# A fused attention, two-layer network and gated unit on one core: four PSUM buffers for the first batch's V tiles, and the output weights split inside the gated unit

## The chip, the cores and the metric

The kernel runs on one NeuronCore of a Trainium2 chip. The metric is the device time of one execution in microseconds. The engines are named as in the profile: PE (TensorE matmuls), PEld (its weight loads), DVE (VectorE), ACT (ScalarE), POOL (GpSimd) and SP (SyncE, which here only issues DMAs).

## What is computed

Three stages follow each other: windowed attention over 4 batches, 8 heads, 576 positions and head size 64; a layer norm with a two-layer network (512 to 2048 to 512, ReLU, residual); and a gated unit. The part of the reference that this change touches is the gated unit:

```
h = x @ w_in
h = 0.5 * h * (1.0 + np.tanh(c * (h + 0.044715 * h ** 3)))
u, v = h[..., :512], h[..., 512:]
v_n = (v - mu) / np.sqrt(var + 1e-06) * g_ln
v_s = np.einsum('ts,bsd->btd', w_sg, v_n) + b_sg[None, :, None]
return x + (u * v_s) @ w_out
```

mu and var are taken over the 512 features of v. x has 4 batches of 576 rows and 512 columns; w_in is 512 x 1024, w_sg 576 x 576, w_out 512 x 512.

## The kernel before, in words

Every product of float32 matrices is made of three products of shorter numbers: each operand is split into a high part (ACT copies it to a rounded type) and a low part (POOL, or DVE, subtracts the high part from the source). The names of these pairs end in h and l. Weights arrive as 64-bit floats and pass a longer split first (class `Split64`): ACT line 76, DVE lines 81, 83, 85 and 88, ACT line 92 for the high part, POOL line 93 for the low part.

**Phase 1** (`phase1`) does attention and the two-layer network. A planner (`Sched`) plays the engines forward with assumed costs and priorities and so writes the order of instructions on each engine. The last work of phase 1 on PE are the products of line 796 into the tiles `acc` (two halves of 12 matmuls each for the last piece), which DVE scales (line 735, `et`) and adds to x (line 739); two DMAs (line 742) bring that x to DRAM. It is the ninth group of rows, and it holds the last 64 rows ("tail") of all four batches.

**Phase 2** (`Phase2`) is the gated unit. Its weights are loaded and split by jobs (`Job`), in the order wv, wu, the first rows of x, ws, wo. When attention is over, `end_attention` hands all jobs to the planner (`flow`), so that their steps fill gaps of phase 1. It also hands it two early V tiles (`early_v`): V tile i is the product of 128 rows of x with wv, 12 matmuls of 512 columns on line 1037 (`v_products`), into one of the two buffers of the PSUM pool `ps_v`. The constants `EPRI` place these two among the last steps of phase 1.

Behind phase 1 the order is that of the code (`Phase2.run`). `play` takes a list of chunks. For each it issues the chunk's matmuls, then one further step of every chunk that is still pending, then so many ticks of the job queue (`tick`: at most one step of each active job, and one new load). The chunks are

- `v_tile`, three steps: *first* (ACT square line 1069, DVE line 1070, ACT tanh line 1071), *stats* (DVE lines 1074, 1088, 1089, 1090, then POOL's power on line 1091) and *norm* (DVE line 1094, then the split into vn: ACT line 1028, POOL line 1029). Line 1074 is the last reader of the PSUM buffer. V tile 4 is the tail of two batches; its parts are called vt.
- `u_chunk`, 24 matmuls on line 1113 over all 576 rows of x, in a buffer of the pool `ps_u` (three buffers); then the same *first*, and DVE line 1074 into u.
- `vs_chunk` (SG), 28 matmuls on line 1130 into a `ps_u` buffer, each chunk reading all of vn and vt; then DVE lines 1134 and 1137 (the gate) and a split into gh and gl.
- `out_chunk` (O), 24 matmuls on line 1158 from gh, gl and wo, then DVE line 1164 and the DMA of the output.

`first_tail` splits the tail of batch 0 straight from SBUF: into x2h and x2l (64 rows, read by every U chunk) and into xth and xtl (128 rows, read by V tile 4). For batch 1 and later the rows of x come back from DRAM by jobs (`x2_jobs`, `tail_jobs`), which queue behind wo's. Of batch 0 the order of chunks is V0 V1, then `first_tail`, then V2 V3 U0 V4 U1 U2 U3 with two ticks behind each, then SG 0 to 3 with two ticks each.

Of the kernel before, what the change touches and what calls it, by code (L numbers as in the profile page):

```python
# [7 lines left out]
F32 = mybir.dt.float32  # L8
# [6 lines left out]
PSUM = bass.MemoryType.PSUM  # L15
# [3 lines left out]
DM, DF, DG = 512, 2048, 512  # L19
# [24 lines left out]
LBACK = 14, 26  # L44
OB, OC = 3, 0
LQ = 1, 0, 3, 2, 4, 8
EPRI = (-1, 9)

NF = 3
SNAKE = ((0, 0), (1, 0), (1, 1), (0, 1), (2, 0), (2, 1), (2, 2), (0, 2), (1, 2), (1, 3), (0, 3), (2, 3))  # L50
# [14 lines left out]
class Split64:  # L65
# [25 lines left out]
    def last(self, h, l):  # L91
        self.nc.scalar.activation(out=h, in_=self.x, func=ACTF.Copy)
        self.nc.gpsimd.tensor_tensor(out=l, in0=self.x, in1=h.bitcast(F32), op=ALU.subtract)
# [105 lines left out]
class Unit:  # L199


    def __init__(self, run, i):
        self.run, self.i = run, i
        self.last = i == run.i1 - 1
# [17 lines left out]
def phase1(tc, nc, a, x2d, cst, p2):  # L222
# [99 lines left out]
    need = {}  # L322
# [520 lines left out]
    def end_attention():  # L843
        yield Op(None, 0, 0, need=[("ev", s.n) for s in runs] + [("w", n) for n in range(40)], token="attention")
        for p in (P["st"], raw, ap2, ps_s, ps_o, ps_t):
            p.release()
        p2.ps_v = tc.alloc_tile_pool(name="ps_v", bufs=2, space=PSUM, side="right", reuse_waits="tile")
        p2.open_0()
        sched.done["p2", "wv"] = sched.now
        for n, j in enumerate(list(p2.queue)):  # L850
            sched.spawn(p2.flow(sched, j, n), sched.now)
        for i in range(2):
            sched.spawn(p2.early_v(i, when[2, stream[-1]] + EPRI[i]), sched.now)

    for e in units:
# [3 lines left out]
    for gen in ([warm(), constants()] + [load_wide(slice(x, y), t) for x, y, t in LW]  # L859
                + [moe(), open_split(), last_quarter(), end_attention()]  # L860
                + [weights(n) for n in range(40)] + [norm(g) for g in range(G)]
                + [load(s) for s in runs if not s.wide] + [scores(s) for s in runs] + [burst(s) for s in runs if s.n >= KB] + [unit(e) for e in units]):
        sched.spawn(gen)
# [41 lines left out]
class Phase2:  # L905
# [122 lines left out]
        nc.scalar.activation(out=h, in_=src, func=ACTF.Copy)  # L1028
        nc.gpsimd.tensor_tensor(out=l, in0=src, in1=h.bitcast(F32), op=ALU.subtract)  # L1029

    def v_products(self, i):
        xs = self.xtail if i == 4 else self.x
        c0 = 0 if i == 4 else i * 128
        ps = self.ps_v.tile([128, DG], F32, tag="v", name="ps_v")
        for kc in range(4):
            for x, (s, m) in enumerate(((0, 0), (0, 1), (1, 0))):
                self.nc.tensor.matmul(ps, xs[s][:, kc, c0:c0 + 128], self.wv[m][:, kc], start=kc == 0 and x == 0,  # L1037
                                      stop=kc == 3 and x == 2)
        return ps

    def early_v(self, i, pri):

        yield Op("PE", 2560, pri, need=[("sc2", n) for n in range(4)] + [("st2", 8)])
        self.early[0, i] = self.v_products(i)

    def run(self, x8, left):
        tc, nc, a, x2d = self.tc, self.nc, self.a, self.x2d
        wu, wo, ws, xtail, bb, g2 = self.wu, self.wo, self.ws, self.xtail, self.bb, self.g2
# [3 lines left out]
        vn = self.pair(wp, [128, 4, DG], "vn")  # L1052
        tp = self.open("p2a", 3)
        bp = self.open("p2b")
        ps_u = tc.alloc_tile_pool(name="ps_u", bufs=3, space=PSUM, reuse_waits="tile")
        self.vt = {}
        K1 = 0.044715
        KC = float(np.sqrt(2.0 / np.pi))
# [1 line left out]
        def gelu2(ps, shape):  # L1060

            t = tp.tile([128, S], F32, tag="ge", name="ge")
            n = int(np.prod(shape))
            t = t[:, :n]
            if len(shape) == 2:
                t = t.rearrange("p (a b) -> p a b", a=shape[0])

            def first():
                act.activation(out=t, in_=ps, func=ACTF.Square)
                dve.scalar_tensor_tensor(out=t, in0=t, scalar=1.0 / K1, in1=ps, op0=ALU.add, op1=ALU.mult)  # L1070
                act.activation(out=t, in_=t, func=ACTF.Tanh, scale=K1 * KC)  # L1071

            def last(out):
                dve.scalar_tensor_tensor(out=out, in0=t, scalar=1.0, in1=ps, op0=ALU.add, op1=ALU.mult)

            return first, last

        def v_tile(b, i):

            ps = self.early.pop((b, i)) if (b, i) in self.early else self.v_products(i)  # L1080
            first, last = gelu2(ps, [DG])
            t = tp.tile([128, DG], F32, tag="vg", name="vg")
            ag = tp.tile([128, 2], F32, tag="ba", name="ba")

            def stats():
                st = tp.tile([128, 6], F32, tag="bs", name="bs")
                last(t)
                dve.bn_stats(out=st, in_=t)
                dve.bn_aggr(out=ag, in_=st)
                dve.tensor_scalar(ag[:, 1:2], ag[:, 1:2], 4e-6, None, ALU.add)  # L1090
                pool.tensor_tensor(out=ag[:, 1:2], in0=ag[:, 1:2], in1=mh, op=ALU.pow)

            def norm():
                dve.tensor_scalar(t, t, ag[:, 0:1], ag[:, 1:2], ALU.subtract, ALU.mult)
                if i < 4:
                    self.split(vn[0][:, i], vn[1][:, i], t)
                else:
                    for z in range(2):
                        o = self.vt[b + z] = self.vtp[z]
                        hi, lo = slice(64 * z, 64 * z + 64), slice(64 - 64 * z, 128 - 64 * z)  # L1100
                        self.split(o[hi], o[lo], t[hi])

            return [first, stats, norm]
# [68 lines left out]
        def play(chunks, ticks=1):  # L1172


            for f, b, i in chunks:
                pend.append(f(b, i))
                for st in pend:
                    st.pop(0)()
                pend[:] = [st for st in pend if st]
                for z in range(ticks):  # L1180
                    self.tick()

        V = lambda b: [(v_tile, b, i) for i in range(5 if b % 2 == 0 else 4)]
        U = lambda b: [(u_chunk, b, d) for d in range(4)]
        SG = lambda b: [(vs_chunk, b, d) for d in range(4)]
        O = lambda b: [(out_chunk, b, d) for d in range(4)]
        play(V(0)[:2])
        self.first_tail(x8)
        for p in left:
            p.release()  # L1190
        gp = self.open("p2g", 2)
        load_res(0)
        self.need("wu")
        play([V(0)[2], V(0)[3], U(0)[0], V(0)[4]] + U(0)[1:], 2)
        self.need("ws")
        for b in range(B):
            nb = b + 1
# [10 lines left out]
            v, o = V(nb), O(b) if nb < B - 1 else []  # L1208
# [78 lines left out]
```

## Time and profile before

| what | value |
|---|---|
| median of three runs | 754.61 us (753.49 to 755.19) |
| the profiled execution's own time | 752.81 us |
| its span in the profile | 750.8 us |
| PE busy | 736.4 us, 98% of the span |
| DVE, ACT, POOL busy | 448.3, 308.5, 245.8 us |
| PE's share of the chain that ended last | 93% |

Busy time is the time in which an engine had an instruction in work, and PE's matmuls overlap, so that a matmul of 0.39 us can follow the one before after 0.23 us. The clock (PEclk) is the share of full speed that TensorE was granted. Times in the rows are microseconds from the start of the span.

### The profile page before, as it was taken

Reading aid. Unit: us, or ns where it says so; the run is one execution under the profiler, and the core shown is the slowest. Engines: PE = TensorE matmul, PEld = TensorE weight load, DVE = VectorE, ACT = ScalarE, POOL = GpSimd, SP = SyncE. Lnnn points to the kernel's source line nnn. Section 1 sums busy time; section 2 is a strip of 40 time slices with the busy share of each in tenths; the row PEclk is TensorE's granted clock in tenths of the full one; section 3 lists DMA queues with packets and bytes.
Section 4 is the critical chain, followed back from the end, with each engine's and each line's share of the span. In section 5 each row is a group of like instructions: output and inputs, shape, how many; then the busy total and the mean of one; then the engine's idle time right before and its main releaser. Section 6 shows DMA issues by size and latency. Waiting matters only on the chain.

```text
span 750.8 us, 15850 instructions
## 1 busy us (share of the span) xinstructions
PE 736.4 (98%) x6270; PEld 685.9 (91%) x6270; DVE 448.3 (60%) x1149; ACT 308.5 (41%) x795; POOL 245.8 (33%) x307
## 2 busy tenths in 40 slices
PE   7999999999999999999999999999899999999998
PEld 3669899999999999999999999999799999999997
DVE  6899889896643453453343438434966746647632
ACT  5896755544323323433323424233453334243410
POOL 2533432333313212222212423026356307327220
PEclk9999999999999999999999999999999999999999
DMA  8654631331121020021122234304500050160002
GB/s 296 220 176 117 190 106 34 92 106 51 56 89 52 25 69 26 27 85 29 28 66 58 71 90 131 124 30 139 183 24 2 31 173 0 48 206 0 1 33 94
DMA packets 51625, 63.41 MB, mean 84 GB/s; under 512 B 10336, under 2 KB 38880, under 8 KB 51552
## 3 DMA queue, kind: packets, MB, share of 16 engines
q1 hardware_dynamic: 51552, 62.41, 26.5%
q8 instruction: 49, 0.80, 0.4%
q14 instruction: 24, 0.20, 0.1%
HBM read 52.96 MB, written 9.44 MB: 83 GB/s over the span
## 4 chain that ended last, share of the span: by engine, by line
PE 93%; DVE 2%; DMA 1%; ACT 1%; POOL 1%; issue 1%; SPq 0%; DVEq 0%; POOLq 0%; ACTq 0%
PE ps_h L785 26%; PE acc L796 25%; PE ps_s L1130 8%; PE ps_u L1113 7%; PE ps_o L1158 7%; PE ps_v L1037 6%; PE o L622 5%; PE tps L582 3%; PE s L454 3%; PE ps_ln L701 1%; DMA st<-in_w 1%; PE ps_ln L644 1%; DMA st<-in_wo 1%; PE ps_w L356 1%; PE s L440 1%
## 5 line engine op out<-in xcount | busy, mean ns | idle before, releaser
L796 PE MATMUL acc<-hh,w2h 128*128 128x256 f32 x576 | 163.6, 284 | 0.0
L785 PE MATMUL ps_h<-xh,w1h 128*128 128x256 f32 x576 | 163.0, 283 | 0.0
L785 PE MATMUL ps_h<-xl,w1h 128*128 128x256 f32 x576 | 160.2, 278 | 0.0
L785 PE MATMUL ps_h<-xh,w1l 128*128 128x256 f32 x576 | 160.1, 278 | 0.0
L796 PE MATMUL acc<-hl,w2h 128*128 128x256 f32 x576 | 160.1, 278 | 0.0
L796 PE MATMUL acc<-hh,w2l 128*128 128x256 f32 x576 | 160.0, 278 | 0.0
L726 DVE SCALAR_TENSOR_TENSOR hl<-ps_h,hh 128x512 fp32r<-128x512 f32 x72 | 49.7, 690 | 127.3 <-ACT hh L724 127.0
L785 PEld LDWEIGHTS ps_h<-xh,w1h 128*128 128x128 f32 x576 | 108.6, 188 | 1.0 <-issue 0.9
L796 PEld LDWEIGHTS acc<-hh,w2h 128*128 128x128 f32 x576 | 108.7, 189 | 0.7 <-DVE sc L85 0.3
L796 PEld LDWEIGHTS acc<-hl,w2h 128*128 128x128 f32 x576 | 108.4, 188 | 0.2
L785 PEld LDWEIGHTS ps_h<-xl,w1h 128*128 128x128 f32 x576 | 108.4, 188 | 0.1
L785 PEld LDWEIGHTS ps_h<-xh,w1l 128*128 128x128 f32 x576 | 108.3, 188 | 0.0
L796 PEld LDWEIGHTS acc<-hh,w2l 128*128 128x128 f32 x576 | 108.3, 188 | 0.0
L724 ACT ACTIVATE hh<-ps_h 128x512 fp32r<-128x512 f32 x72 | 42.8, 595 | 138.8 <-PE ps_h L785 138.8
L463 POOL TENSOR_SCALAR_AFFINE_SELECT m<-m 128x256 f32<-128x256 f32 x100 | 44.7, 452 | 143.7 <-ACT m L543 141.6
L505 ACT ACTIVATE t<-t,sm 128x128 f32<-128x128 f32 x144 | 56.1, 394 | 14.6 <-DVE sm L499 14.6
L513 POOL TENSOR_TENSOR t<-t,sm 128x256 f32<-128x256 f32 x52 | 32.9, 633 | 42.4 <-DVE sm L509 34.9
L76 ACT ACTIVATE sc<-st 128x512 f32<-128x512 f32 (+1 forms) x52 | 30.9, 599 | 24.6 <-DMA st<-in_w 6.7
L1029 POOL TENSOR_TENSOR gl<-gt,gh 128x576 fp32r<-128x576 f32 x16 | 22.9, 1429 | 53.0 <-ACT gh L1028 53.0
L1071 ACT ACTIVATE ge<-ge 128x512 f32<-128x512 f32 (+1 forms) x34 | 22.4, 657 | 34.9 <-DVE ge L1070 34.9
L85 DVE SCALAR_TENSOR_TENSOR sc<-st,sc 128x512 int32<-128x512 int32 (+1 forms) x52 | 35.9, 692 | 0.3
L622 PE MATMUL o<-m,rv 128*64 128x128 f32 (+3 forms) x416 | 34.7, 296 | 0.3 <-POOL m L463 0.3
(163 smaller groups left out, 1530.5 us busy)
## 6 DMA issues: line engine op xcount, KB each, us to landing
st<-in_w SPq DMA_DIRECT2D x24, 512.0 KB, 4.2
x2d<-x SPq DMA_DIRECT2D x18, 256.0 KB, 2.0
out<-xr SPq DMA_DIRECT2D x15, 288.0 KB, 2.1
st<-in_w SPq DMA_DIRECT2D x16, 256.0 KB, 2.6
st<-in_wi SPq DMA_DIRECT2D x8, 512.0 KB, 3.9
st<-x2d SPq DMA_DIRECT2D x8, 512.0 KB, 5.1
xr<-x2d SPq DMA_DIRECT2D x8, 512.0 KB, 6.3
rq<-in_q SPq DMA_DIRECT2D x28, 128.0 KB, 3.2
```

The source lines that it names most:

```text
L85: dve.scalar_tensor_tensor(out=xi, in0=self.wh, scalar=-0x40000000, in1=xi, op0=ALU.bitwise_and, op1=ALU.bitwise_or)
L463: pool.affine_select(out=out, in_=in_, pattern=pat, compare_op=ALU.is_ge, fill=0.0, base=-1 if up else 0, channel_multiplier=1 if up else -1)
L505: act.activation(out=t[:, h], in_=t[:, h], func=ACTF.Exp, bias=st[:, h:h + 1], scale=-1.0, accum_out=sums[:, h, 0:1])
L622: pe.matmul(s.O[64 * h:64 * h + 64, oc:oc + w], v, s.M[m][0:k, h, mc:mc + w], start=x == 0, stop=x == len(mm) - 1, skip_group_check=True)
L724: act.activation(out=h, in_=ps, func=ACTF.Relu)
L726: dve.scalar_tensor_tensor(out=l, in0=ps, scalar=0.0, in1=h.bitcast(F32), op0=ALU.max, op1=ALU.subtract)
L785: pe.matmul(ps[:, half], w[:, kc, f], m[:, kc], start=kc == 0 and x == 0, stop=kc == 3 and x == 2)
L796: pe.matmul(accs[half][:, d], w[:, f, ds], m[:, k], start=fi and d == 0 and k == 0 and x == 0, stop=la and k == 1 and x == 2, skip_group_c ...
L1037: self.nc.tensor.matmul(ps, xs[s][:, kc, c0:c0 + 128], self.wv[m][:, kc], start=kc == 0 and x == 0, stop=kc == 3 and x == 2)
L1113: pe.matmul(ps[:, z, 0:288], wu[s][:, kc, ds], self.x[m][:, kc, 288 * z:288 * z + 288], start=kc == 0 and x == 0, stop=kc == 3 and x == 2)
L1130: pe.matmul(ps[:, z, 0:288], l, r[:, 288 * z:288 * z + 288], start=n == 0, stop=n == len(mm) - 1)
L1158: pe.matmul(ps[:, z, 0:288], wo[s][:, kc, ds], gated[b][m][:, kc, 288 * z:288 * z + 288], start=n == 0, stop=n == 11)
```

## The change

- `EPRI` has four entries, so four early V tiles are planned into the end of phase 1: V1, V2 and V3 directly one behind another. Tiles 0 and 1 of batch 0 go to a new PSUM pool `ps_e` of two buffers, tiles 2 and 3 to `ps_v`. V2 and V3 ask for the second part of x as well (`8 + i // 2`).
- `ps_u` is opened later, when `ps_e` has been released; it covers the same banks.
- The four wo jobs are left out of the planner's hands. They stay in the queue of `Phase2` and are done by its ticks, ahead of the jobs for batch 1's x.
- All four V tiles of batch 0 are played before `first_tail`, without ticks. The order behind it is U0 U1 V4 U2 U3.

```
-EPRI = (-1, 9)
+EPRI = (-1, 9, 10, 11)
...
-        for n, j in enumerate(list(p2.queue)):
+        p2.ps_e = tc.alloc_tile_pool(name="ps_e", bufs=2, space=PSUM, side="right", reuse_waits="tile")
+        for n, j in enumerate(z for z in list(p2.queue) if z.name != "wo"):
             sched.spawn(p2.flow(sched, j, n), sched.now)
-        for i in range(2):
+        for i in range(4):
             sched.spawn(p2.early_v(i, when[2, stream[-1]] + EPRI[i]), sched.now)
...
-    def v_products(self, i):
+    def v_products(self, b, i):
...
-        ps = self.ps_v.tile([128, DG], F32, tag="v", name="ps_v")
+        ps = (self.ps_e if b == 0 and i < 2 else self.ps_v).tile([128, DG], F32, tag="v", name="ps_v")
...
-        yield Op("PE", 2560, pri, need=[("sc2", n) for n in range(4)] + [("st2", 8)])
-        self.early[0, i] = self.v_products(i)
+        yield Op("PE", 2560, pri, need=[("sc2", n) for n in range(4)] + [("st2", 8 + i // 2)])
+        self.early[0, i] = self.v_products(0, i)
...
-        ps_u = tc.alloc_tile_pool(name="ps_u", bufs=3, space=PSUM, reuse_waits="tile")
...
-        play(V(0)[:2])
+        play(V(0)[:4], 0)
+        self.ps_e.release()
+        ps_u = tc.alloc_tile_pool(name="ps_u", bufs=3, space=PSUM, reuse_waits="tile")
         self.first_tail(x8)
...
-        play([V(0)[2], V(0)[3], U(0)[0], V(0)[4]] + U(0)[1:], 2)
+        play(U(0)[:2] + V(0)[4:] + U(0)[2:], 2)
```

The first place is ACT's row from the square of V1 to the square of V3 and the tail split. Of before (ps_v_7065 is V1, ps_v_7140 V2, ps_v_7168 V3; x2h<-x and xth<-x are the tail):

```order
L1069 ACTIVATE ge_7113<-ps_v_7065 128x512
L1071 ACTIVATE ge_7113<-ge_7113 128x512
L92 ACTIVATE woh_6935<-sc_7028 128x512
L1028 ACTIVATE x2h_6665<-x_5432 128x4x64
L1028 ACTIVATE xth_6937<-x_5432 128x512
L1028 ACTIVATE vnh_7095<-vg_7107 128x512
L1069 ACTIVATE ge_7153<-ps_v_7140 128x512
L1071 ACTIVATE ge_7153<-ge_7153 128x512
L1028 ACTIVATE vnh_7095<-vg_7114 128x512
L1069 ACTIVATE ge_7181<-ps_v_7168 128x512
```

The same place of ACT with the change (ps_v_7035 is V1, ps_v_7087 V2, ps_v_7115 V3, ps_u_7161 U0):

```order
L1069 ACTIVATE ge_7075<-ps_v_7035 128x512
L1071 ACTIVATE ge_7075<-ge_7075 128x512
L1029 ACTIVATE vnh_7061<-vg_7070 128x512
L1069 ACTIVATE ge_7100<-ps_v_7087 128x512
L1071 ACTIVATE ge_7100<-ge_7100 128x512
L1029 ACTIVATE vnh_7061<-vg_7076 128x512
L1069 ACTIVATE ge_7128<-ps_v_7115 128x512
L1071 ACTIVATE ge_7128<-ge_7128 128x512
L1029 ACTIVATE x2h_6668<-x_5432 128x4x64
L1029 ACTIVATE xth_6936<-x_5432 128x512
L1029 ACTIVATE vnh_7061<-vg_7101 128x512
L1069 ACTIVATE ge_7186<-ps_u_7161 128x576
```

The tail split has moved from behind V1's tanh to behind V3's tanh, and the last wo copy ahead of it is gone.

The second place is DVE between V4's line 1074 and its norm on line 1094. Of before (vg_7249 is V4):

```order
L1074 SCALAR_TENSOR_TENSOR vg_7249<-ge_7248,ps_v_7235 128x512
L1088 BN_STATS bs_7284<-vg_7249 128x6
L1089 BN_AGGR ba_7250<-bs_7284 128x2
L1090 TENSOR_SCALAR ba_7250<-ba_7250 128x1
L1070 SCALAR_TENSOR_TENSOR ge_7283<-ge_7283,ps_u_7258 128x576
L1094 TENSOR_SCALAR vg_7249<-vg_7249,ba_7250 128x512
```

And with the change (vg_7256 is V4; sc_7238 and sc_7265 belong to the first and second piece of wo):

```order
L83 TENSOR_SCALAR sc_7238<-sc_7238 128x512
L85 SCALAR_TENSOR_TENSOR sc_7238<-st_7199,sc_7238 128x512
L1074 SCALAR_TENSOR_TENSOR vg_7256<-ge_7255,ps_v_7242 128x512
L1088 BN_STATS bs_7293<-vg_7256 128x6
L1089 BN_AGGR ba_7257<-bs_7293 128x2
L1090 TENSOR_SCALAR ba_7257<-ba_7257 128x1
L1070 SCALAR_TENSOR_TENSOR ge_7292<-ge_7292,ps_u_7267 128x576
L88 SCALAR_TENSOR_TENSOR sc_7238<-st_7199,sc_7238 128x512
L81 TENSOR_SCALAR sc_7265<-sc_7265 128x512
L83 TENSOR_SCALAR sc_7265<-sc_7265 128x512
L85 SCALAR_TENSOR_TENSOR sc_7265<-st_7201,sc_7265 128x512
L1094 TENSOR_SCALAR vg_7256<-vg_7256,ba_7257 128x512
```

Seven instructions of the wo split (the two of the first piece above, its line 81 ahead of them, and four more) now stand between V4's line 1070 and its norm, where there was none.

The third place is ACT during SG, where batch 1's x is split. Of before (gh<-gt are the four gates, x2h<-st the parts of batch 1's x):

```order
L1028 ACTIVATE gh_7358<-gt_7389 128x576
L1028 ACTIVATE x2h_6665<-st_7393 128x4x256
L1028 ACTIVATE gh_7358<-gt_7426 128x576
L1028 ACTIVATE x2h_6665<-st_7395 128x4x256
L1028 ACTIVATE gh_7358<-gt_7464 128x576
```

With the change:

```order
L92 ACTIVATE woh_6934<-sc_7308 128x512
L1029 ACTIVATE gh_7353<-gt_7384 128x576
L92 ACTIVATE woh_6934<-sc_7351 128x512
L1029 ACTIVATE x2h_6668<-st_7391 128x4x256
L1029 ACTIVATE gh_7353<-gt_7427 128x576
L1029 ACTIVATE x2h_6668<-st_7396 128x4x256
L1029 ACTIVATE gh_7353<-gt_7468 128x576
```

The first part of batch 1's x now stands behind the last piece of wo, and that piece's DVE steps stand behind the first two gates.

## Rows read from the trace of the kernel before

**Rows 1.** The page's first part: busy us (share of the span) and instructions.

```profile
PE 736.4 (98%) x6270; PEld 685.9 (91%) x6270; DVE 448.3 (60%) x1149; ACT 308.5 (41%) x795; POOL 245.8 (33%) x307
```

**Rows 2.** PE's waits, whole span: us in total, times, longest.

```profile
PE ps_v L1037 <- DVE vg L1074: 3.2, 1, 3.2
```

**Rows 3.** Timeline of PE: start, us, instruction, idle before and its releaser.

```profile
533.38 0.28 PE L796 MATMUL acc<-hh,w2l 128*128 128x256 f32 x1
...
536.05 0.39 PE L1037 MATMUL ps_v<-wvh,x2l 128*128 128x512 f32 x1
539.68 0.50 PE L1037 MATMUL ps_v<-wvh,x2h 128*128 128x512 f32 x1 [3.25 <-DVE vg L1074]
...
546.89 0.42 PE L1113 MATMUL ps_u<-x2h,wuh 128*128 128x288 f32 x2
```

**Rows 4.** Busy time by stretch: PE, PEld, DVE, ACT, POOL (instructions), PEclk, DMA.

```profile
536.30:539.70 3.40, 0.15 (x2) 0.02 (x1) 3.37 (x6) 2.11 (x4) 1.59 (x1) 1.00 0.51 140
...
540.50:543.90 3.40, 3.40 (x10) 2.63 (x9) 3.09 (x8) 2.50 (x5) 1.83 (x3) 0.50 1.09 386
543.90:546.90 3.00, 3.00 (x15) 2.44 (x14) 0.69 (x1) 1.23 (x2) 3.00 (x4) 1.00 0.61 210
```

**Rows 5.** Timeline of DVE around the first V tiles.

```profile
533.54 0.68 DVE L735 TENSOR_TENSOR et<-acc,rstd 128x512 f32<-128x512 f32 x1
534.26 0.69 DVE L739 TENSOR_TENSOR x<-x,et 128x512 f32<-128x512 f32 x1
...
538.95 0.68 DVE L1074 SCALAR_TENSOR_TENSOR vg<-ge,ps_v 128x512 f32<-128x512 f32 x1
...
542.05 0.69 DVE L1074 SCALAR_TENSOR_TENSOR vg<-ge,ps_v 128x512 f32<-128x512 f32 x1
```

**Rows 6.** Timeline of DVE: V0 of batch 1, nothing else in its way.

```profile
581.77 0.69 DVE L1070 SCALAR_TENSOR_TENSOR ge<-ge,ps_v 128x512 f32<-128x512 f32 x1 [1.24 <-ACT ge L1069]
583.16 0.69 DVE L1074 SCALAR_TENSOR_TENSOR vg<-ge,ps_v 128x512 f32<-128x512 f32 x1 [0.70 <-ACT ge L1071]
```

**Rows 7.** Timelines of ACT and POOL: the tail split into x2h and x2l.

```profile
542.45 0.40 ACT L1028 ACTIVATE x2h<-x 128x256 fp32r<-128x256 f32 x1
...
543.86 0.74 POOL L1029 TENSOR_TENSOR x2l<-x,x2h 128x256 fp32r<-128x256 f32 x1
```

**Rows 8.** The chain that ended last: start, us, what.

```profile
547.05 3.19 PE ps_u L1113 x24
...
562.63 14.93 PE ps_s L1130 x112
577.56 5.45 PE ps_v L1037 x24
```

**Rows 9.** Timeline of DVE: steps of the wo split, the last one beside a POOL instruction.

```profile
524.51 0.43 DVE L81 TENSOR_SCALAR sc<-sc 128x512 f32<-128x512 f32 x1 [3.17 <-ACT sc L76]
...
525.44 0.69 DVE L85 SCALAR_TENSOR_TENSOR sc<-st,sc 128x512 int32<-128x512 int32 x1
...
528.37 1.49 DVE L85 SCALAR_TENSOR_TENSOR sc<-st,sc 128x512 int32<-128x512 int32 x1
```

**Rows 10.** Timeline of POOL: low parts of wo, of vt, and of batch 1's x.

```profile
528.02 1.30 POOL L93 TENSOR_TENSOR wol<-sc,woh 128x512 fp32r<-128x512 f32 x1 [3.64 <-ACT woh L92]
...
560.88 2.65 POOL L1029 TENSOR_TENSOR vt<-vg,vt 64x512 fp32r<-64x512 f32 x2 [1.33 <-ACT vt L1028]
...
570.42 2.38 POOL L1029 TENSOR_TENSOR x2l<-st,x2h 128x1024 fp32r<-128x1024 f32 x1
```

**Rows 11.** Timeline of DVE: V4's line 1070, its norm, and a gate beside POOL.

```profile
555.66 0.69 DVE L1070 SCALAR_TENSOR_TENSOR ge<-ge,ps_v 128x512 f32<-128x512 f32 x1 [0.42 <-ACT ge L1069]
...
559.59 0.55 DVE L1094 TENSOR_SCALAR vg<-vg,ba 128x512 f32<-128x512 f32 x1
...
570.99 2.44 DVE L1137 TENSOR_TENSOR gt<-gt,u 128x576 f32<-128x576 f32 x1
```

**Rows 12.** Timeline of ACT: the high part of batch 1's first rows.

```profile
568.80 1.04 ACT L1028 ACTIVATE x2h<-st 128x1024 fp32r<-128x1024 f32 x1
```

More of the change, by code (lines that the diff above doesn't have):

```diff
@@ L1078, in v_tile @@
         def v_tile(b, i):
-            ps = self.early.pop((b, i)) if (b, i) in self.early else self.v_products(i)
+            ps = self.early.pop((b, i)) if (b, i) in self.early else self.v_products(b, i)
             first, last = gelu2(ps, [DG])
```

## The prediction

> **What bounds the kernel now.** The page's first part comes first: PE is busy for 736.4 of 750.8 us [rows 1], so time can be won only where PE stands still or runs slowly, and lost by any new stop. The list of PE's waits is next: it has one entry in the gated unit, 3.2 us on V tiles for DVE's line 1074 [rows 2]. The timeline shows where: V1's last matmul starts at 536.05, V2's first at 539.68, after 3.25 us of nothing [rows 3]. V2 needs the PSUM buffer of V0, whose last reader, line 1074, runs from 538.95 to 539.63 [rows 5]. The table by stretch shows a second loss: after that stop the granted clock is 0.50 (1.2 GHz) from 540.5 to 543.9, with 10 matmuls in 3.40 us, where the next stretch has 15 in 3.00 at 1.00 (2.4 GHz) [rows 4]. V1's twelve matmuls took 2.77 us (533.50 to 536.28); V2 and V3 took 7.21, from 539.68 to U0's start at 546.89 [rows 3], so the clock cost 7.21 - 2 x 2.77 = 1.65 us. Stop and clock together are 4.9 us, and that is all that this change can win.
>
> From 546.89 on the chain that ended last is PE alone: U chunks of 3.19 us, four SG chunks in 14.93, two V tiles in 5.45 [rows 8]. A stop put into it goes to the end in full.
>
> **The change, part by part.**
>
> *Four buffers.* V2 and V3 find their buffers empty and their rows of x were split long before. V1 starts at 533.50 (the matmul before it starts at 533.38 [rows 3]) and a tile takes 2.77 us, so V3 is done at 541.83. The 3.25 us and the 1.65 us go: -4.9. It adds no matmul and removes none.
>
> *What is late next: the tail of x.* U0 now follows at 541.83. Its first matmul covers rows 0 to 287, its second rows 288 to 575, and those include the tail. The tail split stands on ACT behind V3's tanh (first place of the order), where before it stood behind V1's. So I carry the chain of the V tiles forward. The last acc matmul starts at 533.38 and ends at 533.66 [rows 3]; line 735 and line 739 take 0.72 from start to start and 0.69 more [rows 5], which ends at about 535.1 with no wo step between. V0's line 1070 starts there; from it to line 1074 are 1.39 us [rows 6], so 536.44. From one tile's line 1074 to the next are 3.10 us, 538.95 to 542.05 [rows 5], because each norm waits for POOL's power and the next tile's line 1074 stands behind that norm. Three tiles on, V3's line 1074 starts at 545.75 and its tanh, 0.7 us before it [rows 6], at 545.1. The tail's high part follows at 545.6 and takes 0.40 [rows 7], so PE's second matmul can start at 546.1: 4.15 us of stop. The low part takes POOL 0.74 [rows 7] and is there at 546.9, after another 0.55 with two matmuls between. U0 has lost 4.7 us: +4.7. It is then where it would be had it started at 546.5, against 546.89 before. The new wait takes back nearly all of the old one.
>
> *The clock.* The stop of 3.25 us was followed by a stretch at 1.2 GHz; one of 4.7 us should be too, and it then falls into U0 and U1. I take the same price, +1.65. The bounds are 0, if the clock stays, and twice that, if it falls for two such stretches.
>
> *The wo split, later.* Its four DMAs now stand behind the x2d writes and the xr loads on SP's queue and have the V tiles and U0 to land in. Batch 1's x loads now wait on SP for the wo pieces' buffers; by the chain below the first is free at 563.4, 18 us ahead of the copy that reads it. Both are hidden. Its DVE steps are 2 x 0.43 and 2 x 0.69 for each of four pieces [rows 9], 9.0 us, and where before they lay in phase 1, under acc and V0, they now stand between the steps that free buffers and make vt, gh and batch 1's x. They also meet POOL: a line 85 that takes 0.69 alone took 1.49 beside a POOL instruction that runs from 528.02 to 529.32 [rows 9, 10], and a gate took 2.44 until 573.43 beside one that ends at 572.80 [rows 10, 11]. Each ended 0.54 to 0.63 us after POOL's did. So I let such a step wait for POOL's end and give it all but 0.14 us of its own time behind it. Three places follow.
>
> (1) vt. With U0 back, U1 and V4 behind it and the slow clock, V4's products end at 546.5 + 2 x 3.19 + 2.77 + 1.65 = 557.3, and its line 1070 starts at 558.1, one square later. Before, from there to V4's norm were 3.93 us [rows 11]. Now seven wo steps stand between (second place of the order), 4 x 0.43 + 3 x 0.69 = 3.8 us; one of them meets a wo low part of 1.30 on POOL [rows 10], about 1 us; some 0.8 of old idle is used up. The norm starts at 566.0. The first vt low part came 2.6 us after the norm's start (559.59 to half of the POOL pair that ends at 563.5 [rows 10, 11]), so it is there at 568.6. SG0 starts at 557.3 + 2 x 3.19 = 563.7 and needs vt after 24 of its 28 pairs, 3.2 of its 3.73 us, at 566.9: +1.7.
>
> (2) A buffer. SG2 takes the buffer of U3. U3's last step on DVE stands behind line 88 of the second wo piece, blocked by POOL's vt splits, and the first three steps of the third, blocked by the second's low part: it ends at 573.5, where SG2 would start at 572.8: +0.8.
>
> (3) Batch 1's x. Its high part was made at 568.80 and its low part from 570.42 to 572.80 [rows 10, 12], 4.8 us ahead of V0 of batch 1 at 577.56 [rows 8]. Now it stands behind the last wo piece (third place of the order). The chain on DVE: gate 0 from 573.5 to 575.1, four wo steps with one wait for POOL to 578.3, gate 1 to 580.2, the last line 88 to 580.8; then ACT's wo copy to 581.5 and the x copy, 1.04 [rows 12], to 582.4; POOL's wo low part to 582.85, and the x low part, 2.38 [rows 10] and half a us for a gate, to 585.8. SG now ends at 581.0. V0 of batch 1 waits 1.45 us for the high part and, after two matmuls, 2.85 for the low: +4.3.
>
> Behind that I find no further stop: from batch 1's V tiles on the orders are as before.
>
> **The sum:** -4.9 + 4.7 + 1.65 + 1.7 + 0.8 + 4.3 = +8.25 us. The three wo terms are one chain and are the uncertain ones. If nothing on DVE or POOL ever blocked the other, the same chain gives 0.6, 0 and 1.4 in place of 1.7, 0.8 and 4.3, a sum of +3.45. I take the blocked prices, since every such meeting in the rows was blocked.
>
> The Trainium skill, "SBUF — State Buffer", section "SBUF: two separate sides", calls the port pair that DVE and POOL share an exclusive lock, held for a whole instruction, with the other side fully blocked. The trace has the block, but each time 0.14 us less than a whole one; by the page the sum would be +9.1.
>
> The profiled execution took 752.81 us (span 750.8 and 2.0 around it), 1.8 below the median of the runs, 754.61. The sum is a difference within that execution; I add it to the median: 762.8 us.
>
> **The rivals.** What a measurement can tell from no change is about 0.2%, 1.5 us.
>
> *The clock falls a second time*, in the stop at batch 1's V0 (1.45 and 2.85 us with 0.46 of matmuls between). For it: 3.25 us were enough once. Against: the stop is cut in two. Up to +1.65 more: 764.5.
>
> *The block is whole*: a blocked step keeps all its own time behind POOL's end. Some six meetings lie in the chain above, 0.14 us each: +0.85, 763.65. Against: the line 85 that takes 0.69 alone ended 0.54 after POOL [rows 9, 10].
>
> *The wo split is hidden after all* and only the tail's wait is new: -4.9 + 4.7 + 1.65 = +1.45, 756.1; with the clock up, -0.2, 754.4. For it: DVE is 60% busy and ACT 41% over the span [rows 1]. Against: those are means, and the steps stand in line with the ones that PE waits for.
>
> *Faster:* the tail is ready when U0 comes. Then the stop and the clock's fall go, nothing takes their place, and 754.61 - 4.9 = 749.7 follows if wo is hidden too. This is decided by when the tail is split: at 541.83 for the whole gain; with the wo terms at zero and the clock up, a stop of under 3.4 us, a tail ready before 545.2, would still be a gain of over 0.2%. Against it: V3's products themselves end at 541.83, and the tail split stands behind V3's square and tanh.
>
> *The change doesn't do what it says*: V2 still waits, for the second part of x. Its split lies ahead of ws and V0 in POOL's order, so I give it little; the time would stay near 754.6 with wo's terms on top.
>
> **How the numbers follow.** My forecast, all three stops, has 0.57; with a second fall of the clock 0.13; with a whole block 0.05; the hidden wo split 0.17, of which 0.06 with the clock up; faster 0.05; V2 still waiting 0.03. Faster by over 0.2%: 0.05. Within 0.2%: the 0.06 and 0.03 and nothing else, 0.09. Slower: 0.86. The range goes from 756.0, the hidden split with the clock down, to 766.0, which takes the second fall (764.5), the whole block (0.85 more) and a margin of 0.65; the unblocked chain, 758.1, lies inside. Left out are the faster case, the flat ones and a little above.
>
> **What would show it.** Right: V2 and V3 without a gap behind V1; PE's wait list with U0's line 1113 for ACT's or POOL's x2 tail, 4 to 5 us; clock 0.50 for some 3.4 us behind it; SG0 waiting for vt, and batch 1's first V tile for x2h and x2l of batch 1, at about 582 to 586. Wrong: U0 starting before 545, or SG and batch 1's V0 without a stop; then the wo steps found cover that I denied them. If the U0 stop is there and the time is below 756, the terms of wo are mis-sized; if V2 still waits, the first step is wrong.

## The result, and the profile after

The changed kernel takes 763.89 us (median of 4 runs, 763.40 to 764.62) against 754.73 us for the kernel before, measured beside it (753.49 to 755.19): a ratio of 1.0125, with a 95% interval of 1.0107 to 1.0142. It is slower by 1.25%; 762.8 had been forecast. Its profiled execution took 763.63 us, its span 761.7.

The page's first part of the changed kernel, to be held against [rows 1]:

```profile
PE 740.3 (97%) x6270; PEld 688.4 (90%) x6270; DVE 448.9 (59%) x1149; ACT 309.0 (41%) x795; POOL 245.6 (32%) x307
```

The work is the same, instruction for instruction. The span is 10.9 us longer, PE is busy for only 3.9 us more: the other 7.0 us are stops, and the 3.9 are the same matmuls, more of them at the lower clock (stretches below). PE's waits in the gated unit (us in total, times, longest), which were one line before [rows 2]:

```profile
PE ps_u L1113 <- ACT x2h L1029: 4.1, 1, 4.1
PE ps_v L1038 <- POOL x2l L1030: 2.5, 1, 2.5
PE ps_s L1130 <- POOL vt L1030: 1.5, 1, 1.5
PE ps_v L1038 <- ACT x2h L1029: 1.0, 1, 1.0
PE ps_s L1130 <- DVE u L1074: 0.8, 1, 0.8
PE ps_u L1113 <- POOL x2l L1030: 0.3, 1, 0.3
```

The wait of V2 for line 1074 is gone, and six others stand in its place. PE's timeline shows where (the last brackets are the idle time before, and who ended it):

```profile
541.84 0.29 PE L1113 MATMUL ps_u<-x2h,wuh 128*128 128x288 f32 x1
546.22 0.41 PE L1113 MATMUL ps_u<-x2h,wuh 128*128 128x288 f32 x1 [4.09 <-ACT x2h L1029]
...
547.03 0.40 PE L1113 MATMUL ps_u<-x2l,wuh 128*128 128x288 f32 x1 [0.28 <-POOL x2l L1030]
...
568.72 0.54 PE L1130 MATMUL ps_s<-wsh,vt 128*128 128x288 f32 x2 [1.53 <-POOL vt L1030]
...
574.03 0.50 PE L1130 MATMUL ps_s<-wsh,vnh 128*128 128x288 f32 x2 [0.79 <-DVE u L1074]
...
582.78 0.50 PE L1038 MATMUL ps_v<-wvh,x2h 128*128 128x512 f32 x1 [1.05 <-ACT x2h L1029]
...
586.00 0.80 PE L1038 MATMUL ps_v<-wvh,x2l 128*128 128x512 f32 x1 [2.49 <-POOL x2l L1030]
```

U0 starts at 541.84 where it had started at 546.89 [rows 3], does one matmul, and stands until the tail is there. The releasers are on ACT and POOL:

```profile
545.23 0.63 ACT L1071 ACTIVATE ge<-ge 128x512 f32<-128x512 f32 x1 [1.28 <-DVE ge L1070]
545.76 0.40 ACT L1029 ACTIVATE x2h<-x 128x256 fp32r<-128x256 f32 x1
...
581.15 0.63 ACT L92 ACTIVATE woh<-sc 128x512 fp32r<-128x512 f32 x1 [3.89 <-DVE sc L88]
581.69 1.04 ACT L1029 ACTIVATE x2h<-st 128x1024 fp32r<-128x1024 f32 x1
```

The first pair is V3's tanh and the high part of the tail behind it; before, that part was made at 542.45 [rows 7]. The second pair is the last piece of wo and batch 1's x behind it, 12.9 us later than before [rows 12]. On POOL, the low parts of wo, of vt and of batch 1's x:

```profile
564.30 1.29 POOL L93 TENSOR_TENSOR wol<-sc,woh 128x512 fp32r<-128x512 f32 x1 [1.32 <-ACT woh L92]
567.41 2.62 POOL L1030 TENSOR_TENSOR vt<-vg,vt 64x512 fp32r<-64x512 f32 x2 [1.82 <-ACT vt L1029]
571.39 1.29 POOL L93 TENSOR_TENSOR wol<-sc,woh 128x512 fp32r<-128x512 f32 x1 [1.36 <-ACT woh L92]
...
583.08 2.87 POOL L1030 TENSOR_TENSOR x2l<-st,x2h 128x1024 fp32r<-128x1024 f32 x1
```

And DVE beside it, wo steps (lines 85 and 88) ahead of V4's norm (line 1094) and of U3's last step (line 1074):

```profile
564.39 1.75 DVE L85 SCALAR_TENSOR_TENSOR sc<-st,sc 128x512 int32<-128x512 int32 x1
566.06 0.54 DVE L1094 TENSOR_SCALAR vg<-vg,ba 128x512 f32<-128x512 f32 x1
...
569.30 1.28 DVE L88 SCALAR_TENSOR_TENSOR sc<-st,sc 128x512 int32<-128x512 int32 x1
...
571.42 1.81 DVE L85 SCALAR_TENSOR_TENSOR sc<-st,sc 128x512 int32<-128x512 int32 x1
573.15 0.74 DVE L1074 SCALAR_TENSOR_TENSOR u<-ge,ps_u 128x576 f32<-128x576 f32 x1
```

In these rows a DVE step waits three times for a POOL instruction that runs beside it, and ends 0.55 us after it (566.14 against 565.59, 570.58 against 570.03, 573.23 against 572.68). Behind the last one U3's step ends, and SG2 starts.

The clock, by stretch (busy time of PE, PEld, DVE, ACT, POOL, then PEclk, DMA share, GB/s):

```profile
547.40:550.80 3.40, 3.40 (x17) 3.40 (x16) 0.28 (x2) 0.00 (x0) 2.56 (x3) 0.50 0.00 0
550.80:554.20 3.40, 3.40 (x27) 3.40 (x27) 1.52 (x3) 1.68 (x3) 0.00 (x0) 1.00 0.00 0
584.90:591.80 6.90, 5.80 (x14) 4.54 (x15) 2.16 (x2) 1.51 (x3) 6.90 (x5) 0.51 0.00 0
```

There are two slow stretches at 1.2 GHz. The first, 3.4 us, is like the one before [rows 4]. The second, behind the stops of 1.05 and 2.49 us at batch 1's x, lasts 6.9 us, of which PE works in 5.8.

By PE's stages (first matmul to first matmul, before and after): V1 to U0 13.39 and 8.21, a gain of 5.18; the four U and V4 15.58 and 22.00, a loss of 6.42; SG until batch 1's first V tile 14.93 and 18.94, 4.01; the two V tiles of batch 1 5.45 and 11.02, 5.57. With 0.13 ahead of V1 that is 10.95, the whole difference of the spans. The idle times above do not hold all of it: in SG they add up to 3.37 us (1.53, 0.79 and 1.05) of the 4.01. Matmuls overlap there, a pair starting every 0.27 us where it takes 0.42; across a stop they do not, so each stop costs some 0.2 us more than its idle time.

### The profile page after: what moved, and what is told of

Read it like the earlier page. It is cut to its first block, busy times and chain, and to the rows that moved or that the text cites. A ratio compares the mean times of both kernels' runs of the same rounds, so it can differ in the third digit from the quotient of the medians.

```text
span 761.7 us, 15853 instructions
## 1 busy us (share of the span) xinstructions
PE 740.3 (97%) x6270; PEld 688.4 (90%) x6270; DVE 448.9 (59%) x1149; ACT 309.0 (41%) x795; POOL 245.6 (32%) x307
## 4 chain that ended last, share of the span: by engine, by line
PE 90%; DVE 4%; ACT 2%; POOL 2%; issue 1%; DVEq 0%; POOLq 0%; ACTq 0%
PE ps_h L785 26%; PE acc L796 26%; PE ps_o L1158 7%; PE ps_u L1113 6%; PE ps_s L1130 6%; PE ps_v L1038 5%; PE o L622 4%; PE tps L582 3%; PE s L454 3%; PE ps_ln L701 1%; PE ps_ln L644 1%; DVE sc L85 1%; DVE ge L1070 1%; PE s L440 1%; POOL x2l L1030 0%
## 5 line engine op out<-in xcount | busy, mean ns | idle before, releaser
L85 DVE SCALAR_TENSOR_TENSOR sc<-st,sc 128x512 int32<-128x512 int32 (+1 forms) x52 | 38.4, 741 | 0.4
```

What stands on the lines that cost most here:

```text
L85: dve.scalar_tensor_tensor(out=xi, in0=self.wh, scalar=-0x40000000, in1=xi, op0=ALU.bitwise_and, op1=ALU.bitwise_or)
```

## The experiments

The table has, for every kernel, the median, its ratio to the kernel before with the 95% interval, and a length from its profiled execution: from V1's first matmul to the first matmul of batch 0's O. That length leaves out what lies ahead of V1, whose first matmul comes at 533.5 to 534.9 us in these profiles, 1.4 us apart at most.

| kernel | median, us | ratio (95%) | V1 to O, us |
|---|---|---|---|
| before | 754.73 | 1 | 49.35 |
| the change | 763.89 | 1.0125 (1.0107 to 1.0142) | 60.17 |
| 1 wo early | 757.57 | 1.0057 (1.0045 to 1.0070) | 54.08 |
| 2 tail first | 759.27 | 1.0074 (1.0060 to 1.0087) | 55.14 |
| 3 both | 751.55 | 0.9973 (0.9962 to 0.9984) | 48.86 |
| 4 wo late alone | 759.47 | 1.0078 (1.0063 to 1.0092) | 56.09 |
| 5 both, old order | 751.62 | 0.9973 (0.9962 to 0.9984) | 46.63 |
| 6 wo early, stop filled | 755.75 | 1.0033 (1.0020 to 1.0046) | 51.66 |
| 7 four buffers alone | 752.61 | 0.9993 (0.9984 to 1.0002) | 48.86 |
| 8 the change, last stop filled | 762.36 | 1.0108 (1.0093 to 1.0124) | 58.00 |
| 9 tail behind V0 | 749.83 | 0.9950 (0.9936 to 0.9964) | 46.42 |
| 10 and one wo piece late | 749.01 | 0.9934 (0.9921 to 0.9948) | 45.11 |

The kernel before was measured beside each group of runs, and its median lay between 753.24 and 754.73; the ratios are the numbers to compare.

**1. The wo split early again.**

```
-        for n, j in enumerate(z for z in list(p2.queue) if z.name != "wo"):
+        for n, j in enumerate(list(p2.queue)):
```

> The changed kernel, but the wo split is again in the planner's hands, in the gaps of phase 1 as before. Theory: the stops in SG and at batch 1's first V tile come from the late wo split alone, so they go (1.53, 0.79, 1.05 and 2.49 us in the changed kernel), and with them the slow clock at 586 to 591. But the wo steps now stand among the steps of the first V tiles on DVE, V3's tanh comes some 2.5 us later, the tail split stands behind it, and U0's stop grows from 4.1 to some 6.5 us. Sum: about 757, between 755 and 759. Rival A, the place of the wo split is harmless and only the tail's place costs: SG keeps its stops from some other work, and the time is 764 to 766. Rival B, the four tiles in a row and the new order of U and V4 cost by themselves: over 761.

757.57 us, within the theory's range. PE's list of waits has one line left in the unit:

```profile
PE ps_u L1113 <- ACT x2h L1029: 6.7, 1, 6.7
```

The clock in and behind that stop (PE, PEld, DVE, ACT, POOL, then PEclk) is at 1.2 GHz for 10.2 us:

```profile
546.10:550.00 3.90, 0.00 (x0) 0.00 (x0) 3.62 (x8) 2.53 (x6) 1.77 (x2) 0.50 0.36 118
550.00:556.30 6.30, 6.27 (x25) 5.96 (x26) 1.42 (x4) 1.01 (x2) 3.71 (x4) 0.50 0.00 0
```

All stops in SG and at batch 1's x are gone with the one line; rival A, which kept them, is out. SG takes 14.93 us and batch 1's two V tiles 5.45, exactly as before [rows 8]. The price is U0's stop, 6.67 us, and the slow clock behind it: wo's steps delay V3's tanh and the tail behind it, so that U0's second matmul starts 15.2 us after V1's first, where it was 12.6 in the change. So the three wo terms of the forecast belong to the late wo split, and U0's stop does not.

**2. The tail split ahead of the first V tile's chain.**

```
+        self.first_tail(x8)
         play(V(0)[:4], 0)
...
-        self.first_tail(x8)
```

> The changed kernel, but the tail of x is split ahead of the first V tile's chain. Theory: U0's stop (4.09 and 0.28 us) and the slow clock behind it go, PE reaches SG0 some 6 us earlier, but vt, the buffer of U3 and batch 1's x come from a chain on DVE, ACT and POOL that the wo split fills and that is hardly earlier than it was; so SG0 waits some 4 us for vt in place of 1.5, and the stops behind it stay near 0.8, 1.0 and 2.5. Sum: 760 to 762, a gain of only 2 to 4 us over the changed kernel. Rival A, the stop of U0 and its clock are a cost of their own: the whole 6.4 us come back, 757 to 758. Rival B, the tail's place has nothing to do with it, U0 waits for something else: 763 to 765.

759.27 us, a little under the theory's range. PE's waits:

```profile
PE ps_s L1130 <- POOL vt L1030: 4.0, 1, 4.0
PE ps_v L1038 <- POOL x2l L1030: 2.5, 1, 2.5
PE ps_v L1038 <- ACT x2h L1029: 0.5, 1, 0.5
```

U0's stop is gone, U0 to SG0 takes 15.57 us (6.43 less than in the change), and SG0 gives 2.5 us of that back at once: its wait for vt is 3.99 in place of 1.53. The last stop is 2.50 us, in the change 2.49. The stops behind U0 are therefore not its consequence: they are deadlines of the chain that wo fills. The wait for U3's buffer, which the theory kept, is gone. The last stop is as long as in the change, but the slow stretch behind it is not:

```profile
583.70:587.10 3.40, 3.40 (x9) 2.67 (x8) 0.01 (x1) 0.69 (x1) 3.40 (x2) 0.50 0.00 0
```

Batch 1's two V tiles take 9.97 us here and 11.02 in the change, where that stretch lasted 6.9 us.

**3. Both put back**, so that the four buffers, the four tiles in a row and the order U0 U1 V4 U2 U3 remain.

> The changed kernel with both parts put back: the wo split in the planner's hands, and the tail split ahead of the first V tile's chain. What is left of the change are the four buffers, the four V tiles in a row and the order U0 U1 V4 U2 U3. Theory: no stop is left from V0 to batch 1's V tiles and the clock does not fall there, so the time is that of before less the 4.9 us of V2's stop and its slow clock: 749 to 751. Rival A, with V2's stop gone PE simply reaches the next thing that is late (the tail split, a buffer of U, vt), and a stop of 2 to 4 us with its own fall of the clock stands there: 752 to 755. Rival B, the four buffers or the order of the chunks cost by themselves: over 755.

751.55 us, faster than before by 0.27%, between the ranges of the theory and of rival A. One stop is left:

```profile
PE ps_s L1130 <- POOL vt L1030: 2.6, 1, 2.6
```

By its mechanism it is rival A: with V2's stop gone PE meets the next late thing, vt, with 3.4 us of slow clock behind it. In the nine runs the clock over the whole span was 0.997 or 0.998 in four (749.52 to 750.85 us) and 0.992 or 0.995 in five (751.55 to 752.98).

**4. The late wo split alone**, on the kernel before.

```
-        for n, j in enumerate(list(p2.queue)):
+        for n, j in enumerate(z for z in list(p2.queue) if z.name != "wo"):
```

> The kernel before, with one part of the change alone: the wo split is taken out of the planner's hands and done by the ticks of the gated unit. Theory: at V0 it helps, since no wo step stands in DVE's order between the last steps of phase 1 and V0's chain: V0's line 1074 comes some 2.5 us earlier and V2's stop shrinks from 3.25 to some 0.7 us. Behind that it costs as in the changed kernel: SG0 waits for vt, a buffer of U, batch 1's x. Sum: 756 to 759. Rival A, the place of the wo split is harmless: only the gain at V2 is left, 751 to 754. Rival B, the late split costs only because U0's stop has shifted the chain in the changed kernel: then no stop in SG here, and again 751 to 754.

759.47 us, just above the theory's range. The first half holds: V2's stop shrinks from 3.25 to 0.73 us. The second half comes at another place:

```profile
567.85 0.82 PE L1130 MATMUL ps_s<-wsh,vnh 128*128 128x288 f32 x2 [7.71 <-DVE u L1074]
```

DVE in that kernel, from U1's line 1070 to its line 1074, which frees SG0's buffer, with steps of wo's third and fourth piece and V4's norm between:

```profile
562.69 0.74 DVE L1070 SCALAR_TENSOR_TENSOR ge<-ge,ps_u 128x576 f32<-128x576 f32 x1
563.35 0.68 DVE L88 SCALAR_TENSOR_TENSOR sc<-st,sc 128x512 int32<-128x512 int32 x1
563.95 0.42 DVE L81 TENSOR_SCALAR sc<-sc 128x512 f32<-128x512 f32 x1
564.41 0.43 DVE L83 TENSOR_SCALAR sc<-sc 128x512 int32<-128x512 int32 x1
564.87 1.72 DVE L85 SCALAR_TENSOR_TENSOR sc<-st,sc 128x512 int32<-128x512 int32 x1
566.51 0.53 DVE L1094 TENSOR_SCALAR vg<-vg,ba 128x512 f32<-128x512 f32 x1
566.97 0.74 DVE L1074 SCALAR_TENSOR_TENSOR u<-ge,ps_u 128x576 f32<-128x576 f32 x1
```

DVE does not stand still here: it is a line of steps, and the one that PE waits for is the last. Here nothing held PE at U0, so the one stop at SG0 takes it all. The clock is 0.50 from 563.3 to 573.5, 5.7 us of it behind the stop, and SG takes 17.5 us, 2.6 more than before. Batch 1's x is in time, with 5.49 us for two V tiles. The late wo split needs no late tail to cost more than V2's stop did.

**5. Run 3 with the chunks in the order of the kernel before.**

```
-        play(U(0)[:2] + V(0)[4:] + U(0)[2:], 2)
+        play([U(0)[0], V(0)[4]] + U(0)[1:], 2)
```

> The run with both parts put back, and the order of the chunks put back too: U0 V4 U1 U2 U3, so that of the change only the four buffers and the four V tiles in a row are left, with the tail split ahead of them. Theory: the stop of 2.59 us at SG0 in the run before came from V4 standing one U chunk later than in the kernel before, so that vt was late once V2's stop had gone; with V4 back, vt is some 3 us earlier, the stop and the 1.7 us of slow clock behind it go, and the time is 747 to 750. Rival A, vt is held by DVE's and ACT's lines, not by when V4 is multiplied: the stop stays at 2 us or more, 751 to 752. Rival B, U1 or a buffer of U is late instead: a new stop of 1 to 3 us before SG0, 750 to 752.

751.62 us: the theory's time was missed. Its mechanism held, since no stop is left in SG; but a new one stands ahead of V4, which needs V2's buffer, nearest to rival B:

```profile
547.58 0.50 PE L1038 MATMUL ps_v<-wvh,xth 128*128 128x512 f32 x1 [1.96 <-DVE vg L1074]
```

The clock did not fall there. From V1 to O this is 2.2 us shorter than run 3, but the medians are equal. Run 3's profile is of the slowest of its nine executions (752.98 us), run 5's of one that is 0.95 us under its median, so the two lengths do not compare the medians; how much the order itself brings stays open.

**6. Run 1 with U0's stop filled by useless matmuls** into the buffer that U0's first matmul overwrites.

```
+            for r in range(48 if (b, d) == (0, 0) else 0):
+                pe.matmul(ps[:, 0, 0:288], wu[0][:, 0, ds], self.x[0][:, 0, 0:288], start=True, stop=True)
```

> The run with the early wo split (757.6 us, U0's stop 6.67 us with 6.5 us at 1.2 GHz behind it), with useless work in the stop: ahead of U0's matmuls PE multiplies its first one 48 times more, into U0's buffer, which U0's own first matmul then overwrites. That adds some 6.4 us of matmuls and needs nothing that the stop waits for. Theory: the tail is no earlier, so U0's second matmul starts when it did; but PE does not stand still, the clock does not fall, and the 3.3 us that the clock cost come back: 754 to 755. Rival A, the clock falls there whatever PE did before: 757 to 758. Rival B, PE then reaches SG0 3.3 us earlier and waits there for vt: 756 to 757.5, with a stop of 2 us or more at SG0.

755.75 us, 0.24% less than run 1 by the ratios, with 48 matmuls more. That lies above the theory's range and below both rivals'. Two stretches, the filled stop and what follows it (columns as in run 1):

```profile
542.50:549.10 6.60, 6.60 (x50) 6.37 (x48) 6.06 (x13) 3.86 (x8) 3.61 (x4) 1.00 0.70 245
550.00:553.00 3.00, 2.71 (x21) 2.69 (x21) 0.91 (x3) 0.47 (x1) 3.00 (x4) 1.00 0.00 0
```

PE stands still for only 0.35 and 0.29 us, for the tail's high and low part, the clock stays at 2.4 GHz, and U0 and U1 take 13.88 us in place of 16.31. The tail comes when it did: U0's second matmul starts 6.96 us after the chunk's first in both runs. So the fall of the clock has a price of its own, here 2.4 us. The theory had 3.3; at the full clock PE waits for the low part, and in run 1, at half the clock, it did not.

**7. The four buffers alone.**

```
-        play(V(0)[:4], 0)
+        play(V(0)[:2])
+        self.first_tail(x8)
+        play(V(0)[2:4], 2)
         self.ps_e.release()
         ps_u = tc.alloc_tile_pool(name="ps_u", bufs=3, space=PSUM, reuse_waits="tile")
-        self.first_tail(x8)
```

together with runs 1 and 5's edits.

> Of the change the four buffers alone: V0 to V3 in a row on PE, everything else as in the kernel before (tail split behind V1's tanh, wo split in the planner's hands, order U0 V4 U1 U2 U3, ticks). Theory: V2's stop goes, and U0 comes 4.9 us earlier than the tail, which ACT and POOL split at 542.45 and 543.86 in the kernel before; so U0's second and third matmul wait some 1 to 3 us in all, and the clock may fall behind that. Sum: 751 to 754. Rival A, the tail is ready in time: 748 to 750. Rival B, the four buffers cost by themselves, through a buffer or a bank that is held longer: over 754.5.

752.61 us, as the theory had it, and no change (0.9993, 0.9984 to 1.0002). PE's waits:

```profile
PE ps_u L1113 <- ACT x2h L1029: 1.6, 1, 1.6
PE ps_u L1113 <- POOL x2l L1030: 1.2, 1, 1.2
PE ps_v L1038 <- DVE vg L1074: 1.2, 1, 1.2
```

The 3.25 us before V2 have become 1.56, 1.20 and 1.15 us at U0 and V4. The buffers only move PE's wait, because the chain of steps that makes the tail and frees the buffers is no shorter: V0's line 1074 starts 6.1 us after V1's first matmul, 5.5 in the kernel before.

**8. The change with its last stop filled.**

```
+        for r in range(10 if (b, i) == (1, 0) else 0):
+            self.nc.tensor.matmul(ps, xs[0][:, 0, c0:c0 + 128], self.wv[0][:, 0], start=True, stop=True)
```

> The changed kernel, with useless work in its last stop: ahead of the first V tile of batch 1 PE multiplies that tile's first product (rows of x2h by wvh) 10 times more, some 2.3 us, into the tile's own buffer, which its first matmul then overwrites. It needs x2h alone, so the wait for x2l (2.49 us in the changed kernel) is nearly filled, and x2l is no earlier. Theory: what followed that stop, PE at 1.2 GHz from 584.9 to 591.8, cost 2.9 us by itself and came because PE stood still; without it the time is 760.5 to 761.5. Rival A, the clock falls anyway, on the waits of SG0, SG2 and x2h ahead of it: 763 to 764.5, with a slow stretch at the same place. Rival B, PE's earlier arrival only meets the next thing that is late (a buffer of batch 1, gh and gl): 762 to 763.5 with a new stop behind it.

762.36 us, above the theory's range and in that of rival B, but the new stop of rival B is not there. At the place itself the theory holds, and the slow stretch is gone (stretches behind U0's stop and at batch 1's x, columns as in run 1):

```profile
545.90:552.80 6.90, 5.60 (x22) 5.29 (x23) 2.54 (x6) 1.98 (x4) 4.10 (x5) 0.51 0.22 90
584.20:588.00 3.80, 3.52 (x14) 2.65 (x15) 3.77 (x3) 2.35 (x4) 3.80 (x3) 1.00 0.01 2
```

Batch 1's two V tiles take 8.41 us, the useless work included, in place of 11.02: 2.6 us back. But in this execution the first slow stretch, behind U0's stop of 4.08 us, lasts 6.9 us where the change's profile has 3.4. Over the whole span all four runs of this kernel had a clock of 0.993, and the four of the change 0.991 (the profiled one) and 0.989, so the gain at the clock is not that of one execution alone.

**9. and 10. Towards a faster kernel.** Run 5 with the tail split behind V0's square (9), and with the last of the four wo pieces left to the ticks (10):

```
+        play(V(0)[:1], 0)
         self.first_tail(x8)
-        play(V(0)[:4], 0)
+        play(V(0)[1:4], 0)
...
-        for n, j in enumerate(list(p2.queue)):
+        for n, j in enumerate(list(p2.queue)[:-1]):
```

> The run with the four buffers, the early wo split and the order of the kernel before (751.6 us, a stop of 1.96 us at V4, which waits for V2's line 1074), but with the tail split behind V0's square instead of ahead of it. Theory: in that run V0's square stood behind the two copies of the tail on ACT, and DVE then waited 0.89 us for it; now the square comes first, all V steps come 0.6 to 0.9 us earlier, V4's stop shrinks to 1.0 to 1.4 us, and the tail is still ready when U0's second matmul comes. The time falls by 0.5 to 1 us: 750.5 to 751.2. Rival A, DVE's wo steps set V0's start: no change, 751.6. Rival B, the tail is late for U0 by 0.5 us or more: 751.5 to 752.5.

> The run with the tail behind V0's square, and of the four pieces of wo the last one taken out of the planner's hands and done by the ticks of the gated unit, three pieces as before. Theory: what makes V2's line 1074 late for V4 are wo steps among the last steps of phase 1; with one piece less there V0's chain starts some 1.5 to 2.5 us earlier and V4 does not wait, and the one late piece (2.2 us on DVE) stands between U0 and U3, where vt had 2 us to spare. So no stop is left before batch 1: 748 to 750. Rival A, one late piece already makes vt or a buffer of U late: a stop of 1 us or more in SG, 750.5 to 752.5. Rival B, the V chain starts no earlier, being held by the other pieces: V4's stop stays, 751 to 752.

Run 9: 749.83 us, lower than forecast, but hardly for the reason given. V4's stop is 1.71 us where 1.0 to 1.4 was expected, and V1 to O is only 0.2 us shorter than in run 5. V0's line 1074 comes 0.5 us earlier behind V1's first matmul than in run 5 and V2's only 0.2, because POOL's tail split now delays the power for V0's norm, for which DVE waits 0.48 us. Of the 0.8 us between the two profiled executions 0.5 lie ahead of V1, where nothing was changed. Most of the step from 751.62 is not explained by these rows.

Run 10: 749.01 us, in the theory's range, 0.66% faster than the kernel before and 1.9% faster than the change; its interval overlaps run 9's. V4 does not wait, and the one stop is

```profile
PE ps_s L1130 <- DVE u L1074: 0.5, 1, 0.5
```

V0's line 1074, which frees the first of the V buffers in `ps_e`, starts 3.8 us after V1's first matmul; in run 5 that was 6.5. This is DVE in run 10 around it:

```profile
534.80 0.68 DVE L735 TENSOR_TENSOR et<-acc,rstd 128x512 f32<-128x512 f32 x1
535.52 1.07 DVE L739 TENSOR_TENSOR x<-x,et 128x512 f32<-128x512 f32 x1
536.51 0.67 DVE L1070 SCALAR_TENSOR_TENSOR ge<-ge,ps_v 128x512 f32<-128x512 f32 x1
537.88 0.69 DVE L1074 SCALAR_TENSOR_TENSOR vg<-ge,ps_v 128x512 f32<-128x512 f32 x1 [0.70 <-ACT ge L1071]
```

No wo step stands between the last steps of phase 1 and V0's. With the chain shorter the four buffers bring, from V1 to O, 4.2 us of the 4.9 that V2's stop and its slow clock had cost.

## Why the prediction was right, and where its sum was off

- *V2's stop.* Forecast -4.9, by PE's stages -5.18. U0 started at 541.84; 541.83 was forecast.
- *The tail late for U0.* Forecast 4.15 and 0.55 us, measured 4.09 and 0.28. V3's tanh was forecast at 545.1 and started at 545.23. The chain of V steps was carried to the right place, and runs 1 and 2 show that it is the tail's place on ACT: with wo early the stop grows, with the tail first it goes.
- *The clock behind it.* Forecast 1.65, measured 2.05 (the 6.42 us that the U stage lost, less 4.37 of stops; it holds what two stops cost beyond their idle time).
- *vt, U3's buffer.* Forecast 1.7 and 0.8 (0.7 by its own two times, 573.5 and 572.8), measured 1.53 and 0.79. vt was there at 568.7, for 568.6.
- *Batch 1's x.* Forecast 1.45 and 2.85, measured 1.05 and 2.49.
- *The blocked price.* The steps beside POOL ended 0.55 us after it, 0.14 less than the 0.69 they take alone, as the sum had it. The Trainium skill, "SBUF — State Buffer", section "SBUF: two separate sides", has the other side fully blocked; these three meetings agree with the block, but not with a whole one.
- *What was mis-sized: the clock at batch 1's x.* The sum has no term for it. The prediction had it as a rival, with a chance of 0.13 and "up to +1.65 more", and held against it that the stop is cut in two. The clock did fall there, for 6.9 us, so that batch 1's two V tiles lost 3.1 us beside the stop of 2.49 (11.02 - 5.45 - 2.49). Run 8 shows that PE's standing still brought it about: with the stop filled, the stretch is gone and 2.6 us come back. Behind the same stop in run 2 the tiles lost only 2.0 us, near the rival's price; why the stretch was twice as long in the change stays open.
- *What no term had.* The stops of SG cost 0.64 us more than their idle time.

So the places and the stops were right within half a us each, and the sum in the profile was not: +8.25 against +10.9. That 762.8 came within 1.1 us of 763.89 is in part luck: the medians differ by only 9.2, because the profiled execution of before was 1.9 us under its median of 754.73 and that of after 0.26 under. Of the rivals, the hidden wo split falls by runs 1 and 4, the faster case by U0's stop of 4.09 us, V2 still waiting by the list of waits, and the whole block by the 0.55 us. Run 7 adds that the buffers alone change nothing measurable.

Not tried: taking POOL out of DVE's way, which would price the blocked steps by themselves.

## What to carry to other kernels

Before a buffer is added to remove a wait, follow the engine that was waited for: if its line of steps is no shorter, the next user of that line waits instead (run 7). With the same four buffers a gain came when the tail moved forward in the line (0.27% in run 5, 0.50% in run 9), and the lowest median when steps left it (0.66% in run 10). Work that has no deadline of its own still has a place in an in-order queue: by busy shares DVE, at 60%, could hide the wo split anywhere, and yet moving it alone cost 0.78% (run 4), because of the steps that stood behind it. And a stop on TensorE is to be priced with what the clock does behind it, which can be as much as the stop itself (run 8: 2.6 us came back behind a stop of 2.49).

## What was not expected of the hardware

Slow stretches at 1.2 GHz were not of one length: 3.4 us behind stops of 3.25 and 2.59 us (before and run 3), 3.4 us behind 2.50 in run 2 and 6.9 us behind 2.49 at the same place in the change, 10.2 us around stops of 6.67 and 7.71 (runs 1 and 4), where 6.3 and 5.7 us of it lay in PE's work. With a stop of 4.1 us it was 3.4 us in one execution and 6.9 in another, where it began before the stop was over (the change and run 8). No fall followed the stops of 1.96 and 1.71 us in the profiles of runs 5 and 9. Where the clock fell the stage lost, beside the stop, about half of the part in which PE worked: 3.3 us in run 1, 3.1 at batch 1's V tiles. Filling a stop with useless matmuls kept the clock up both times it was tried, and gave back 2.4 and 2.6 us.
